# Weight preparation moved to GpSimd, one sum moved from GpSimd to VectorE, and weight loads placed otherwise, in a three-layer attention and mixing kernel

## The chip, the cores and the metric

One core of one Trainium2 chip. The metric is the device time of one execution in microseconds (us). TensorE is PE in the profile, its weight loads PEld, VectorE DVE, ScalarE ACT, GpSimd POOL, SyncE (which issues the DMAs) SP.

## What is computed

Eight batches of 576 tokens with 512 channels go through an attention with pooled keys and values, a mixing layer, and a second mixing layer, which is where the change lies:

```python
def _moe2_ref(x, w_tok1, w_tok2, w_ch1, w_ch2):     # x: 8 x 576 x 512
    xt = x.transpose(0, 2, 1)
    h = np.maximum(xt @ w_tok1, 0.0) @ w_tok2        # 576 -> 256 -> 576
    u = x + h.transpose(0, 2, 1)
    h2 = np.maximum(u @ w_ch1, 0.0) @ w_ch2          # 512 -> 1536 -> 512
    return u + h2
```

The first mixing layer ends with `u + np.maximum(u @ w_ch, 0.0)`. All weights arrive as 64-bit floats, two 32-bit words each, and are converted to fp32 by the kernel.

## The kernel before

A Tile program: instructions are written in source order, with priorities, and a scheduler places them on each engine as their inputs come ready, so that the order on an engine is not that of the source. All matrix products are made of a high and a low part of each operand (three products for one), and the two large products of the last layer use a Strassen-like scheme of seven block products, named A11, S2, A12, S1, S3, S4 and A22, so that sums and differences of the weight blocks have to be made first.

The stages, in us from the start of the span: attention and the first mixing up to about 547. From 547 to 777 the **token stage**: for each batch, eight (j, th) products with their evacuation into u on DVE (`emit_ch`, L878: relu of the product plus u), a copy of u's last 64 tokens (`dup_tail`, L536), transposes of u on PE (`emit_tr`, L173), their evacuation on ACT and DVE, and two token products (`emit_tok1`, `emit_tok2`, L927, with the store of the result to DRAM). From 777 to 1067 the **first channel product**: 36 iterations of `first_pair` (6 chunks of tokens by 6 blocks of channels), each of seven products of six matmuls. Product A11 is made in bank X and copied to p1 by ACT (L1252); S2 in Y, added to p1 by DVE as u2 (L1256); A12 is accumulated on X, its relu is the block g11 (ACT, L1260); S1 in W, copied to p5 by ACT (L1265); S3 in Z, added to p5 by DVE (L1268), then u2 added to p5 by POOL (L1269) and the relu taken by ACT (L1270); S4 on W gives g12 (L1274 DVE, L1275 ACT), A22 on Z gives g21 (L1279 DVE, L1281 ACT). Four blocks go to DRAM (L1246). Between the products, `pump` prepares operands of the next chunk: differences on DVE (L1118) and splits into high (ACT, L1114) and low parts (DVE, L1115). From 1067 to the end the second channel product.

The **weights** of the two channel products are prepared beside these stages, in steps taken by `wstep` (one after a piece of other work). `weight_steps(0, ...)` treats w_ch1 in 6 quads of 128x256 blocks, `weight_steps(1, ...)` w_ch2 in 12 quads of 128x128 blocks. A quad is: `load` (SP, L977, into ws), `conv` of its two halves from 64-bit words into wm (Abs on ACT L986, then DVE L987, L988, L992, L996), `sums` into wsum (two on POOL L1005, L1006, two on DVE L1007, L1008), `split` in two halves into wo (cast on ACT L1019, low part L1020 on POOL for the first half and on DVE for the second), and stores of wo to DRAM (L1021). The buffers of ws, wm, wsum and wo rotate over the tags given in the call; for w_ch2 each of them is one buffer (ws and wsum share the tag "kr"). The next quad's load comes after the split. `HOME_S` names the ten buffers that the evacuations of `first_pair` rotate over.

What orders the work besides priorities and the pools is only the data: a step of weights may be placed as early as its inputs are there.

## Time and profile before

| | us |
|---|---|
| median of 3 runs (lowest to highest) | 1337.89 (1337.18 to 1340.5) |
| the profiled execution | 1337.63 |
| its span | 1335.4 |
| mean granted clock of TensorE | 0.992 of 2.4 GHz |
| PE busy | 1278.4 (96%) |
| DVE, ACT, POOL busy | 970.2 (73%), 629.4 (47%), 357.9 (27%) |

The profile is of one execution. All positions are us after the start of its span, which is 2.2 us shorter than the execution's own time. Busy shares are means over stages with different limits, so a stage is read by itself: what PE does there, and what it waits for.

### The profile page before, as it was taken

Reading aid. Unit: us, or ns where it says so; the run is one execution under the profiler, and the core shown is the slowest. Engines: PE = TensorE matmul, PEld = TensorE weight load, DVE = VectorE, ACT = ScalarE, POOL = GpSimd, SP = SyncE. Lnnn points to the kernel's source line nnn. Section 1 sums busy time; section 2 is a strip of 40 time slices with the busy share of each in tenths; the row PEclk is TensorE's granted clock in tenths of the full one; section 3 lists DMA queues with packets and bytes.
Section 4 is the critical chain, followed back from the end, with each engine's and each line's share of the span. In section 5 each row is a group of like instructions: output and inputs, shape, how many; then the busy total and the mean of one; then the engine's idle time right before and its main releaser. Section 6 shows DMA issues by size and latency. Waiting matters only on the chain.

```text
span 1335.4 us, 22306 instructions
## 1 busy us (share of the span) xinstructions
PE 1278.4 (96%) x8214; PEld 1219.0 (91%) x8216; DVE 970.2 (73%) x1721; ACT 629.4 (47%) x1172; POOL 357.9 (27%) x376
## 2 busy tenths in 40 slices
...
GB/s 330 145 87 112 58 99 78 85 91 60 108 64 69 32 85 146 200 245 294 288 72 81 141 217 207 206 221 181 201 226 171 364 315 211 165 186 209 185 94 69
DMA packets 119613, 213.70 MB, mean 160 GB/s; under 512 B 11152, under 2 KB 65936, under 8 KB 119504
## 3 DMA queue, kind: packets, MB, share of 16 engines
...
HBM read 133.60 MB, written 78.64 MB: 159 GB/s over the span
## 4 chain that ended last, share of the span: by engine, by line
PE 60%; DVE 21%; issue 8%; DMA 5%; ACT 3%; POOL 3%; SPq 0%; DVEq 0%; POOLq 0%; ACTq 0%
PE x L159 22%; PE m L159 19%; PE t L159 16%; PE x L173 2%; DMA ws<-w_ch 2%; DVE sm L564 2%; DVE e L553 2%; DVE mx L552 2%; DVE tmp L736 1%; DVE sm L565 1%; POOL wo L1020 1%; DVE R L789 1%; DVE pt L605 1%; POOL wsum L1005 1%; DVE early L261 1%
## 5 line engine op out<-in xcount | busy, mean ns | idle before, releaser
L159 PE MATMUL m<-wtk,Z 128*128 128x256 f32 (+1 forms) x1536 | 247.0, 300 | 8.7 <-DVE R L789 8.3
L159 PEld LDWEIGHTS m<-wtk,Z 128*128 128x128 f32 x1536 | 217.7, 190 | 12.0 <-DVE R L789 8.7
L1269 POOL TENSOR_TENSOR p<-p,u 128x384 f32<-128x384 f32 x36 | 39.4, 1094 | 324.0 <-DVE p L1268 317.7
L751 POOL TENSOR_TENSOR Z<-tmp,Z 128x1024 fp32r<-128x1024 f32 x31 | 74.8, 2413 | 111.1 <-ACT Z L750 111.1
L159 PE MATMUL t<-wth,Xh 128*128 128x256 f32 (+1 forms) x504 | 77.1, 295 | 0.5 <-DVE Xh L536 0.2
L159 PEld LDWEIGHTS t<-wth,Xh 128*128 128x128 f32 x504 | 67.8, 190 | 4.5 <-DVE Xh L536 1.8
L718 DVE SCALAR_TENSOR_TENSOR tmp<-tmp,t 128x512 f32<-128x512 f32 x40 | 27.3, 683 | 55.3 <-ACT tmp L705 55.3
L159 PE MATMUL x<-ope_Xl,wa 128*128 128x384 f32 x336 | 65.4, 336 | 0.2 <-DVE ope_Xl L1115 0.2
L159 PE MATMUL m<-ope_Z,wa 128*128 128x384 f32 x300 | 63.7, 337 | 0.8 <-ACT ope_Z L1114 0.6
L159 PE MATMUL x<-ope_R,wa 128*128 128x384 f32 x312 | 61.8, 338 | 0.5 <-DVE p L1268 0.4
L736 DVE TENSOR_TENSOR tmp<-x,tmp 128x1024 f32<-128x1024 f32 x32 | 39.0, 1219 | 31.1 <-ACT tmp L712 16.0
L159 PE MATMUL x<-bdk,q 128*128 128x144 f32 x320 | 49.2, 309 | 11.1 <-DVE bdk L1410 6.6
L159 PEld LDWEIGHTS x<-ope_Xl,wa 128*128 128x128 f32 x336 | 58.9, 188 | 0.5 <-DVE ope_Xl L1115 0.5
L159 PEld LDWEIGHTS x<-bdk,q 128*128 128x128 f32 x320 | 46.0, 209 | 12.8 <-issue 10.8
L159 PE MATMUL m<-wtk,zt 128*128 128x256 f32 (+1 forms) x192 | 56.8, 296 | 0.0
L159 PE MATMUL x<-ope_Z,wa 128*128 128x384 f32 x276 | 55.6, 338 | 1.3 <-ACT p L1265 1.1
L159 PEld LDWEIGHTS x<-ope_R,wa 128*128 128x128 f32 x312 | 55.1, 188 | 1.2 <-DVE p L1268 1.2
L159 PE MATMUL x<-ope_Xh,wa 128*128 128x384 f32 x264 | 55.1, 341 | 0.3 <-DVE p L1268 0.2
L159 PEld LDWEIGHTS m<-ope_Z,wa 128*128 128x128 f32 x300 | 52.9, 188 | 1.8 <-ACT ope_Z L1114 0.9
L705 ACT ACTIVATE tmp<-t,magic 128x512 f32<-128x512 f32 x40 | 27.3, 684 | 57.0 <-PE t L159 44.3
L159 PE MATMUL t<-ope_Z,wa 128*128 128x384 f32 x252 | 53.6, 335 | 0.0
L569 POOL TENSOR_TENSOR e<-e,sm 128x720 f32<-128x720 f32 x32 | 45.1, 1409 | 31.6 <-DVE sm L568 31.1
...
## 6 DMA issues: line engine op xcount, KB each, us to landing
...
```

Source lines behind the costliest of these rows:

```text
L159: nc.tensor.matmul(out=o, lhsT=l, rhs=r, start=start, stop=stop, skip_group_check=skip)
L173: nc.tensor.transpose(o, i, ident)
L261: nc.vector.scalar_tensor_tensor(out=mu, in0=t[:, :, 1], scalar=0xC0000000, in1=mu, op0=ALU.bitwise_and, op1=ALU.bitwise_or,)
L552: nc.vector.tensor_reduce(out=mx[:, c0:c1, :], in_=v, axis=AX.X, op=ALU.max)
L553: nc.vector.tensor_tensor(out=e[:, c0:c1, 2 * p:2 * p + 2, :], in0=v, in1=mx[:, c0:c1, :].unsqueeze(3).to_broadcast([128, n, 2, 72]), op=A ...
L564: nc.vector.tensor_reduce(out=sm, in_=ep, axis=AX.X, op=ALU.add)
L569: nc.gpsimd.tensor_tensor(out=ep, in0=ep, in1=sm.unsqueeze(3).to_broadcast([128, 5, 2, 72]), op=ALU.mult)
L705: nc.scalar.activation(out=t, in_=pt, func=ACTF.Identity, bias=magic[:, 0:1])
L718: nc.vector.scalar_tensor_tensor(out=t, in0=t, scalar=MAGIC, in1=pt, op0=ALU.subtract, op1=ALU.subtract)
L736: nc.vector.tensor_tensor(out=tmp, in0=px.unsqueeze(1).to_broadcast([128, 2, 512]), in1=tmp, op=ALU.mult)
L751: later(1.0 if lo is nc.vector else 0.0, lambda: lo.tensor_sub(out=zl, in0=zv, in1=zh.bitcast(F32)), tg, zg)
L1269: nc.gpsimd.tensor_tensor(out=p5.t, in0=p5.t, in1=u2.t, op=ALU.add)
```

## The change

Weights: the two sums L1007 and L1008 go from DVE to POOL, and so does the low part of the second half; the casts of w_ch2 go from ACT to POOL, its Abs from ACT to DVE as a bitwise operation. The load of the next quad of w_ch2 is placed after `conv` instead of after `split`; wsum has a buffer of its own ("pl"), taken from `HOME_S`. For w_ch1 the load stays after the split, and gets a gate: POOL copies one element of the u just written into the ws tile, so that a load is behind that u. In `first_pair` the sum of p5 and u2 goes from POOL (after the Z add) to DVE (before the Z add). In the token stage the tail of u is copied by ACT instead of DVE.

Line numbers move: L977 becomes L983, L986 L993 (w_ch1) and L995 (w_ch2), L987, L988, L992, L996 become L998, L999, L1003, L1007, the sums L1005 to L1008 L1016 to L1019, the cast L1030, the low part L1031, p1's copy L1271, the u2 add L1275, the new sum of p5 L1285, the Z add L1288, its relu L1289, the g12 add L1293, the g21 add L1298.

```diff
--- before.py
+++ after.py
@@ -532,8 +532,8 @@
     pt_t = {}
     t1_t = {}
 
-    def dup_tail(t):
-        nc.vector.tensor_copy(out=t[:, :, T:TD], in_=t[:, :, 512:T])
+    def dup_tail(t, copy=nc.vector.tensor_copy):
+        copy(out=t[:, :, T:TD], in_=t[:, :, 512:T])
 
     def emit_sc(b, p):
         q = q_t[b, p // 2][:, p % 2, :]
@@ -876,8 +876,9 @@
                 i += 1
         u = u_t[b][:, j, ts]
         nc.vector.scalar_tensor_tensor(out=u, in0=o, scalar=0.0, in1=u, op0=ALU.max, op1=ALU.add)
+        gate[0] = u[0:1, 0:1]
         if j == 3 and th == 1:
-            dup_tail(u_t[b])
+            dup_tail(u_t[b], nc.scalar.copy)
 
     def emit_tr(b, c):
         u = u_t[b]
@@ -963,11 +964,16 @@
 
         def load(i):
             g, j, h = quads[i]
+            behind = gate[0]
             if whole:
                 t = ws_t([128, 2, 2, wd, 2], U32, f"ws{m}_{i}")
                 t = [t[:, kk] for kk in range(2)]
             else:
                 t = [ws_t([128, 2, wd, 2], U32, f"ws{m}_{i}_{kk}") for kk in range(2)]
+            if behind is not None:
+
+                for x in t:
+                    nc.gpsimd.tensor_copy(out=x[0:1, 0, 0:1, 0].bitcast(F32), in_=behind)
             for kk in range(2):
                 if m == 0:
                     src, r, c0 = w_ch1, (2 * kk + j) * 128, g * 256 + h * wd
@@ -983,7 +989,12 @@
             t = raw[i][0][kk]
             x = raw[i][1][:, kk]
             xu = x.bitcast(U32)
-            nc.scalar.activation(out=x, in_=t[:, :, :, 1].bitcast(F32), func=ACTF.Abs)
+            if m == 0:
+                nc.scalar.activation(out=x, in_=t[:, :, :, 1].bitcast(F32), func=ACTF.Abs)
+            else:
+                nc.vector.tensor_scalar(
+                    out=xu, in0=t[:, :, :, 1], scalar1=0x7FFFFFFF, scalar2=None, op0=ALU.bitwise_and
+                )
             nc.vector.tensor_scalar(out=x, in0=x, scalar1=F64_FLOOR, scalar2=None, op0=ALU.max)
             nc.vector.tensor_scalar(
                 out=xu, in0=xu, scalar1=3, scalar2=0x3FFFFFFF,
@@ -1004,20 +1015,20 @@
             a11, a21, a12, a22 = x[:, 0, 0], x[:, 0, 1], x[:, 1, 0], x[:, 1, 1]
             nc.gpsimd.tensor_tensor(out=s[:, 0], in0=a21, in1=a22, op=ALU.add)
             nc.gpsimd.tensor_tensor(out=s[:, 2], in0=a11, in1=a21, op=ALU.subtract)
-            nc.vector.tensor_sub(out=s[:, 1], in0=s[:, 0], in1=a11)
-            nc.vector.tensor_sub(out=s[:, 3], in0=a12, in1=s[:, 1])
+            nc.gpsimd.tensor_tensor(out=s[:, 1], in0=s[:, 0], in1=a11, op=ALU.subtract)
+            nc.gpsimd.tensor_tensor(out=s[:, 3], in0=a12, in1=s[:, 1], op=ALU.subtract)
 
         def split(i, half):
             x, s = raw[i][1:3]
-            parts = ((x[:, 1], 2, A12, nc.gpsimd), (x[:, 0, 0:1], 1, A11, nc.gpsimd)) if half == 0 else (
-                (s[:, 0:2], 2, S1, nc.vector), (s[:, 2:4], 2, S3, nc.vector))
+            parts = ((x[:, 1], 2, A12), (x[:, 0, 0:1], 1, A11)) if half == 0 else (
+                (s[:, 0:2], 2, S1), (s[:, 2:4], 2, S3))
             g, j, h = quads[i]
             if whole:
                 ow = wo_t([128, 2, 2, 2, wd], F32R, f"wo{m}_{i}_{half}")
-            for n, (src, k, o0, eng) in enumerate(parts):
+            for n, (src, k, o0) in enumerate(parts):
                 o = (ow[:, n] if whole else wo_t([128, 2, 2, wd], F32R, f"wo{m}_{i}_{half}{n}"))[:, 0:k]
-                nc.scalar.copy(out=o[:, :, 0], in_=src)
-                eng.tensor_sub(out=o[:, :, 1], in0=src, in1=o[:, :, 0].bitcast(F32))
+                (nc.scalar.copy if m == 0 else nc.gpsimd.tensor_copy)(out=o[:, :, 0], in_=src)
+                nc.gpsimd.tensor_sub(out=o[:, :, 1], in0=src, in1=o[:, :, 0].bitcast(F32))
                 nc.sync.dma_start(out=scr_w[m][:, g, o0:o0 + k, j, h * 2 * wd:(h + 1) * 2 * wd],
                                   in_=o.bitcast(F32).rearrange("p k a c -> p k (a c)"))
 
@@ -1026,17 +1037,24 @@
 
         steps = []
         for i in range(len(quads)):
+            ahead = []
             if i == 0:
                 steps += [lambda: load(0)] + [nothing] * gaps[0]
-            for f, n in ((lambda i=i: conv(i, 0), gaps[1]), (lambda i=i: conv(i, 1), gaps[2]),
-                         (lambda i=i: sums(i), gaps[3]), (lambda i=i: split(i, 0), gaps[4]),
+            if i + 1 < len(quads):
+                ahead = [lambda i=i: load(i + 1)] + [nothing] * gaps[0]
+            for f, n in ((lambda i=i: conv(i, 0), gaps[1]), (lambda i=i: conv(i, 1), gaps[2])):
+                steps += [f] + [nothing] * n
+            if m == 1:
+                steps += ahead
+            for f, n in ((lambda i=i: sums(i), gaps[3]), (lambda i=i: split(i, 0), gaps[4]),
                          (lambda i=i: split(i, 1), gaps[5])):
                 steps += [f] + [nothing] * n
-            if i + 1 < len(quads):
-                steps += [lambda i=i: load(i + 1)] + [nothing] * gaps[0]
+            if m == 0:
+                steps += ahead
         return steps
 
     wq = []
+    gate = [None]
 
     def wstep(n=1):
         while wq and n > 0:
@@ -1049,7 +1067,7 @@
     HOME_E = (("Z1", 5), ("Xh", 3), ("Xl", 3), ("R0", 3))
     HOME_O = (("R1", 3), ("e", 3), ("Z0", 5))
     HOME_R = (("n0", 1), ("n1", 1), ("n2", 1), ("n3", 1))
-    HOME_S = ["vbh", "vlh", "vbl", "vll", "bdk", "stg0", "stg1", "vlr", "t1", "pl"]
+    HOME_S = ["vbh", "vlh", "vbl", "vll", "bdk", "stg0", "stg1", "vlr", "t1"]
 
     def channel_mix():
         class Units:
@@ -1213,7 +1231,8 @@
                 mm(o, l, r, first and i == 0, last and i == len(seq) - 1, cont)
 
 
-        wq[:] = weight_steps(1, 128, (["kr"], ["n4"], ["kr"], ["vr"]), (2, 2, 2, 2, 3, 0))
+        gate[0] = None
+        wq[:] = weight_steps(1, 128, (["kr"], ["n4"], ["pl"], ["vr"]), (2, 2, 2, 2, 3, 0))
         pump(16)
         for g in range(3):
             for o in PO:
@@ -1263,10 +1282,10 @@
             prod(S1, W, True)
             p5 = evac("p5")
             nc.scalar.copy(out=p5.t, in_=W)
+            nc.vector.tensor_add(out=p5.t, in0=p5.t, in1=u2.t)
             Z = bank_any()[:, 0:NH]
             prod(S3, Z, True)
             nc.vector.tensor_add(out=p5.t, in0=Z, in1=p5.t)
-            nc.gpsimd.tensor_tensor(out=p5.t, in0=p5.t, in1=u2.t, op=ALU.add)
             nc.scalar.activation(out=p5.t, in_=p5.t, func=ACTF.Relu)
             put(3, p5)
             prod(S4, W, False)

```

Three places of the order on an engine. DVE in the token stage, the last products of batch 2 (u_6175 is its u; wm, ws, wsum and wo are weights, the first number behind the name is their quad; Xl belongs to the next batch). Before:

```order
L878 SCALAR_TENSOR_TENSOR u_6175<-x_6587,u_6175 128x256
L992 SCALAR_TENSOR_TENSOR wm_5_7482<-ws_5_1_7451,wm_5_7482 128x512
L996 SCALAR_TENSOR_TENSOR wm_5_7482<-ws_5_1_7451,wm_5_7482 128x512
L878 SCALAR_TENSOR_TENSOR u_6175<-x_6606,u_6175 128x320
L1007 TENSOR_TENSOR wsum_5_7549<-wsum_5_7549,wm_5_7482 128x256
L1008 TENSOR_TENSOR wsum_5_7549<-wm_5_7482,wsum_5_7549 128x256
L878 SCALAR_TENSOR_TENSOR u_6175<-m_6620,u_6175 128x256
L1020 TENSOR_TENSOR wo_5_10_7662<-wsum_5_7549,wo_5_10_7662 128x2x256
L878 SCALAR_TENSOR_TENSOR u_6175<-t_6639,u_6175 128x320
L865 TENSOR_TENSOR Xl<-u_6480,Xh 128x576
L536 COPY u_6175<-u_6175 128x4x64
```

and with the change:

```order
L878 SCALAR_TENSOR_TENSOR u_6175<-x_6591,u_6175 128x256
L1007 SCALAR_TENSOR_TENSOR wm_2_6571<-ws_2_0_6537,wm_2_6571 128x512
L998 TENSOR_SCALAR wm_2_6571<-wm_2_6571 128x512
L999 TENSOR_SCALAR wm_2_6571<-wm_2_6571 128x512
L878 SCALAR_TENSOR_TENSOR u_6175<-x_6610,u_6175 128x320
L1003 SCALAR_TENSOR_TENSOR wm_2_6571<-ws_2_1_6538,wm_2_6571 128x512
L1007 SCALAR_TENSOR_TENSOR wm_2_6571<-ws_2_1_6538,wm_2_6571 128x512
L878 SCALAR_TENSOR_TENSOR u_6175<-m_6624,u_6175 128x256
L878 SCALAR_TENSOR_TENSOR u_6175<-t_6643,u_6175 128x320
```

Quad 5 stood in this batch before, with its sums and low parts on DVE ahead of the last two u; now it is quad 2, of which only the conversion is on DVE, and all of it ahead of the last two u.

DVE in the first channel product, between quads 4 and 5 of w_ch2 (p_9135 is p5 of that iteration, u_9117 its u2). With the change:

```order
L1275 TENSOR_TENSOR u_9117<-t_9105,p_9103 128x384
L1003 SCALAR_TENSOR_TENSOR wm_4_9273<-ws_4_9145,wm_4_9273 128x256
L1007 SCALAR_TENSOR_TENSOR wm_4_9273<-ws_4_9145,wm_4_9273 128x256
L1285 TENSOR_TENSOR p_9135<-p_9135,u_9117 128x384
L1288 TENSOR_TENSOR p_9135<-x_9138,p_9135 128x384
L995 TENSOR_SCALAR wm_5_9485<-ws_5_9344 128x256
L1293 TENSOR_TENSOR g_9157<-x_9128,u_9117 128x384
L998 TENSOR_SCALAR wm_5_9485<-wm_5_9485 128x256
L999 TENSOR_SCALAR wm_5_9485<-wm_5_9485 128x256
L1298 TENSOR_TENSOR g_9167<-x_9138,u_9117 128x384
```

Before, quad 4's sums and low parts stood here, and the sum of p5 with u2 was not on DVE:

```order
L1256 TENSOR_TENSOR u_9269<-t_9256,p_9254 128x384
L1007 TENSOR_TENSOR wsum_4_9334<-wsum_4_9334,wm_4_9263 128x128
L1008 TENSOR_TENSOR wsum_4_9334<-wm_4_9263,wsum_4_9334 128x128
L1268 TENSOR_TENSOR p_9287<-x_9289,p_9287 128x384
L1020 TENSOR_TENSOR wo_4_1_9422<-wsum_4_9334,wo_4_1_9422 128x2x128
L1274 TENSOR_TENSOR g_9311<-x_9280,u_9269 128x384
L1020 TENSOR_TENSOR wo_4_1_9422<-wsum_4_9334,wo_4_1_9422 128x2x128
L1279 TENSOR_TENSOR g_9321<-x_9289,u_9269 128x384
```

The first operation of quad 5 (L995) now stands three rows behind the last conversion of quad 4 (L1007), ahead of both adds of the iteration's end.

POOL in the first channel product, quad 4. Before:

```order
L1269 TENSOR_TENSOR p_9204<-p_9204,u_9186 128x384
L1020 TENSOR_TENSOR wo_4_0_9370<-wm_4_9263,wo_4_0_9370 128x128
L1005 TENSOR_TENSOR wsum_4_9334<-wm_4_9263 128x128
L1006 TENSOR_TENSOR wsum_4_9334<-wm_4_9263 128x128
L1020 TENSOR_TENSOR wo_4_0_9370<-wm_4_9263,wo_4_0_9370 128x2x128
L1269 TENSOR_TENSOR p_9287<-p_9287,u_9269 128x384
```

and with the change:

```order
L1017 TENSOR_TENSOR wsum_4_9378<-wm_4_9273 128x128
L1016 TENSOR_TENSOR wsum_4_9378<-wm_4_9273 128x128
L1018 TENSOR_TENSOR wsum_4_9378<-wsum_4_9378,wm_4_9273 128x128
L1019 TENSOR_TENSOR wsum_4_9378<-wm_4_9273,wsum_4_9378 128x128
L1030 CAST wo_4_0_9416<-wm_4_9273 128x2x128
L1030 CAST wo_4_0_9416<-wm_4_9273 128x128
L1031 TENSOR_TENSOR wo_4_0_9416<-wm_4_9273,wo_4_0_9416 128x2x128
L1031 TENSOR_TENSOR wo_4_0_9416<-wm_4_9273,wo_4_0_9416 128x128
L1030 CAST wo_4_1_9466<-wsum_4_9378 128x2x128 x2
L1031 TENSOR_TENSOR wo_4_1_9466<-wsum_4_9378,wo_4_1_9466 128x2x128 x2
```

POOL has the whole quad after its conversion, and no sum of p5 between the quads.

## Rows read from the trace of the kernel before

**Rows 1.** Stage table: busy us (count) of PE, PE weight loads, DVE, ACT, POOL; granted clock, DMA share, GB/s.

```profile
613.00:618.00 5.00, 0.64 (x6) 0.41 (x5) 4.49 (x7) 2.48 (x5) 2.81 (x3) 1.00 0.33 122
618.00:622.00 4.00, 4.00 (x21) 4.00 (x21) 4.00 (x10) 4.00 (x8) 0.00 (x0) 0.57 1.02 372
...
777.00:1002.00 225.00, 211.35 (x1156) 200.73 (x1155) 160.36 (x302) 122.37 (x266) 57.02 (x73) 0.99 0.62 207
```

**Rows 2.** Waits, 500 to 777 us: waiter, releaser, us in total, times, longest.

```profile
PE t L173 <- DVE u L878: 5.2, 2, 4.4
```

**Rows 3.** Timeline near 617 us: start, duration, engine, line, operation, out<-in [idle before <-releaser].

```profile
615.06 2.13 POOL L1020 TENSOR_TENSOR wo<-wm,wo 128x256 fp32r<-128x256 f32 x2
...
616.10 1.37 DVE L1008 TENSOR_TENSOR wsum<-wm,wsum 128x256 f32<-128x256 f32 x1
...
617.86 0.33 PE L173 MATMUL t<-con,u 128*128 128x128 f32 x1 [4.36 <-DVE u L878]
```

**Rows 4.** Waits, 777 to 1067 us, those of PE.

```profile
PE m L159 <- ACT p L1252: 8.9, 16, 1.6
...
PE x L159 <- ACT p L1265: 4.1, 6, 1.8
```

**Rows 5.** Timeline, the relu L1260, five of its 36.

```profile
780.57 0.49 ACT L1260 ACTIVATE g<-m 128x384 f32<-128x384 f32 x1 [1.59 <-PE m L159]
...
805.01 0.47 ACT L1260 ACTIVATE g<-m 128x384 f32<-128x384 f32 x1
...
1002.07 0.49 ACT L1260 ACTIVATE g<-m 128x384 f32<-128x384 f32 x1
...
1032.50 0.49 ACT L1260 ACTIVATE g<-m 128x384 f32<-128x384 f32 x1 [1.55 <-PE m L159]
...
1061.77 0.49 ACT L1260 ACTIVATE g<-m 128x384 f32<-128x384 f32 x1 [1.55 <-PE m L159]
```

**Rows 6.** Timeline around 890 us, relu of p5 and PE.

```profile
891.39 0.53 ACT L1270 ACTIVATE p<-p 128x384 f32<-128x384 f32 x1 [2.25 <-POOL p L1269]
...
894.43 0.96 PE L159 MATMUL m<-ope_R,wa 128*128 128x384 f32 x4 [0.61 <-ACT p L1252]
```

**Rows 7.** Groups by form, 777 to 1000 us: busy us, mean ns | idle before, releasers.

```profile
L1270 ACT ACTIVATE p<-p 128x384 f32<-128x384 f32 x27 | 14.2, 525 | 33.0 <-POOL p L1269 33.0
...
L1019 ACT CAST wo<-wsum 128x256 fp32r<-128x256 f32 x22 | 8.2, 399 | 8.9 <-DMA scr_w<-wo 8.8
...
L1268 DVE TENSOR_TENSOR p<-x,p 128x384 f32<-128x384 f32 x27 | 15.0, 554 | 26.5 <-PE x L159 18.8 <-ACT p L1265 4.1 <-DMA ws<-w_ch 3.0
...
L1020 DVE TENSOR_TENSOR wo<-wsum,wo 128x256 fp32r<-128x256 f32 x22 | 9.6, 457 | 7.7 <-ACT wo L1019 7.7
...
L988 DVE TENSOR_SCALAR wm<-wm 128x256 uint32<-128x256 uint32 x23 | 7.6, 335 | 0.3
L1008 DVE TENSOR_TENSOR wsum<-wm,wsum 128x128 f32<-128x128 f32 x11 | 6.6, 600 | 0.3
...
L1020 POOL TENSOR_TENSOR wo<-wm,wo 128x256 fp32r<-128x256 f32 x11 | 9.3, 849 | 0.0
...
L1006 POOL TENSOR_TENSOR wsum<-wm 128x128 f32<-128x128 f32 x11 | 5.8, 526 | 0.0
```

**Rows 8.** Groups by form on POOL, whole span, one-input operations.

```profile
L574 POOL COPY pl<-e 128x80 f32<-128x80 f32 x64 | 15.5, 272 | 1.9
...
L225 POOL TENSOR_SCALAR early<-early 128x256 f32<-128x256 f32 x6 | 2.5, 418 | 4.0 <-ACT early L224 3.9
```

**Rows 9.** Timeline, POOL and DVE at 783 us and 871 to 875 us.

```profile
783.37 1.67 POOL L1269 TENSOR_TENSOR p<-p,u 128x384 f32<-128x384 f32 x1 [166.19 <-DVE p L1268]
...
871.12 0.95 DVE L1115 TENSOR_TENSOR opo_Z<-raw_n,opo_e 128x768 fp32r<-128x768 f32 x1
...
873.65 1.02 POOL L1269 TENSOR_TENSOR p<-p,u 128x384 f32<-128x384 f32 x1 [7.04 <-DVE p L1268]
874.31 1.17 DVE L1115 TENSOR_TENSOR opo_Z<-raw_n,opo_Z 128x768 fp32r<-128x768 f32 x1 [0.74 <-ACT opo_Z L1114]
```

## The prediction, made before the changed kernel was run

> **What bounds the kernel now.** I read the stage table first. PE carries every stage, and in two places it is not full [rows 1]. At 613 to 618 us it works 0.64 us of 5 while DVE works 4.49; in the 4 us after that the granted clock is 0.57, most of the time the lower of its two levels (1.2 GHz), so that PE's 4.00 busy us hold 0.57 × 4 = 2.3 us of work at full clock. And from 777 to 1002 us it works 211.35 us of 225. I then read what PE waits for. Up to 777 us it is the evacuation of u on DVE, 4.4 of 5.2 us in one piece [rows 2]. The timeline shows why: DVE is inside the weight sum L1008, 1.37 us long beside two low parts on POOL, and PE's next transpose needs a u that DVE has queued behind it [rows 3]. From 777 us on PE waits for two copies that ACT makes out of PSUM, p1 (L1252, 16 waits) and p5 (L1265, 6 waits) [rows 4].
>
> How much that stage loses is best read as a period, since waits for weight loads of PE and slow matmuls are in it too. L1260 runs once in each of the 36 iterations. From 1032.50 to 1061.77, when the weights are done and no operand is being split, four iterations take 29.27 us, 7.32 each. From 780.57 to 1061.77 there are 35 periods in 281.20 us, against 35 × 7.32 = 256.2: **25.0 us of excess** [rows 5]. The same rows tell what is not due to weights: 1002.07 to 1032.50 has no weight work but splits for the next chunk, 30.43 us for four periods, 1.15 over, and such a change of chunk comes five times (5.8 us); the opening, 780.57 to 805.01, is 24.44 for three periods, 2.5 over, most of it before weights. So about 17 us go with the weight work.
>
> How they go is in the chain around 890 us [rows 6]: ACT's relu of p5 has waited 2.25 us for POOL, which adds u2 to p5; behind the relu ACT still has casts of weights and the next relus, then comes the p1 copy, and PE has waited 0.61 us for it. The same wait of the relu is 33.0 us in 27 iterations, and ACT's casts also wait 8.8 for stores of weights [rows 7]. ACT is in order, so each of these delays the copies behind it.
>
> **The change, part by part.**
>
> *Token stage.* A quad's load now waits for the first u of its own batch, so six quads that stood together in 546 to 619 us go one to a batch. On DVE no sum or low part stands between the u any more, and the last u of the batch follows the one before it directly. This takes away the stall of 4.36 us [rows 3] and the low clock behind it, 4 × (1 − 0.57) = 1.7 us [rows 1]. The other wait for u, 5.2 − 4.4 = 0.8 us [rows 2], I leave. Against it: POOL now does all four sums and all four low parts, eight operations a batch at about 1.07 (L1020 has two in 2.13 [rows 3]), 8.5 us of a batch's (777 − 547) / 8 = 28.8. A u that DVE takes meanwhile may be late, as L1008 was; I charge 0.1 in each of six batches, 0.6. The tail copies move to ACT, which PE does not wait for there: nothing, or what a cast of 128x256 takes there (0.40 [rows 7]) once a batch. Gain **5.5**; between 2 (such waits reappear) and 7 (all go).
>
> *First channel product, ACT.* The relu no longer waits for POOL, since DVE adds u2 first (L1285): ACT loses 33.0 us of waiting and, per quad, two Abs and four casts of about 0.4, with the 8.8 of waiting for stores [rows 7]. PE waits for the p1 and p5 copies behind these, so this is where the 17 us can come back.
>
> *DVE.* Per quad it loses two sums of 0.60 and two low parts of 0.46, 2.1 us, and the wait of 7.7 for ACT's casts; it gains two bitwise operations of about 0.34 (as L988) and in each iteration an add of 0.55 (as L1268) [rows 7]; at 27 iterations to 11 quads that is 0.7 + 1.35 = 2.0. Even. But L1285 stands between the p5 copy and the Z add, and a product later PE wants the bank. A product is 7.32 / 7 = 1.046 us; of that some 0.25 is slack once copy and semaphores are paid.
>
> *POOL.* It loses 1.02 an iteration and gains two sums, two low parts and four casts per quad. A cast is not in the trace on POOL. Bounds: 0.27 (a copy of 128x80) and 0.85 (the two-input low part of the same 128x256); nearest is a one-input operation of 128x256 there, 0.42, which I take [rows 7, 8]. A quad is then 4 × 0.53 (sums) + 3 × 0.42 + 0.30 (casts) + 3 × 0.85 + 0.53 (low parts) = 6.8 us instead of 2.5. Twelve quads now end in 20 iterations, one in 20 × 7.32 / 12 = 12.2 us: POOL can carry it.
>
> *The new wait.* There is one buffer of converted weights. The next quad's first operation, now on DVE (L995), may not start before POOL has made four sums, two casts and two low parts from it: 2.1 + 0.7 + 1.4 = 4.2 us after the last conversion. Between quads 4 and 5 L995 follows that after an add, L1285 and L1288, about 2.75 us, so DVE holds with the g12 and g21 adds queued behind; ACT's relus wait for these, the next p1 copy for the relus. Walking the eleven boundaries so, four have L995 early enough to hold PE, by 0.3, 2.0, 1.25 and 1.45 us; at the others it stands behind the last add of an iteration. **5.0 us**, between 0 and 11 × 2.
>
> *Beside POOL.* A two-input DVE operation with both inputs in SBUF takes longer next to POOL: L1115 takes 0.95 alone and 1.17 where it began inside POOL's 1.02 [rows 9]. L1285 is such an add. 20 iterations with weights × 0.22 = **4.4 us**, from 0 (in the slack) to 12.0 (rival C).
>
> A rule of the Trainium skill (SBUF — State Buffer, "SBUF: two separate sides") speaks against this part: a GpSimd operation that reads SBUF and a DVE operation with two SBUF inputs exclude each other for the whole instruction. By it that L1115 would have ended 0.36 + 0.95 = 1.31 us after its start. The row says 1.17: the trace bears the rule out in direction, not in full.
>
> *Loads a block ahead, nine evacuation buffers for ten.* A load has a whole split to land in. Buffers come round after more than an iteration. Nothing; a load that came late would hold L995 as above.
>
> *Sum.* Of the excess 5.8 + 2.5 + 5.0 + 4.4 = 17.7 stays, a gain of 25.0 − 17.7 = 7.3. With 5.5 that is 12.8; 1337.6 (the profiled execution) − 12.8 = 1324.8, and the median is 0.3 above that execution: **1325 us**. The stages up to 547 us and from 1067 us keep their order and time.
>
> **The rivals.** *B, faster:* neither holds nor POOL's neighbourhood cost anything, because the loads and POOL run ahead of my walk. Splits and opening remain, 8.3: gain 16.7 + 5.5 = 22.2, so 1315.7. For it: weight-free iterations show that nothing else binds PE. Against it: the single buffer.
>
> *C, hardly faster:* L1285 waits for a whole low part in each of 20 iterations, 0.85 less 0.25 of slack, 12.0 in place of 4.4, and the stage keeps 25.3 of its 25.0: 1337.6 + 0.3 − 5.5 + 0.3 = 1332.7. For it: L1008 takes 0.60 on average beside POOL, longer than the low part of twice its size (0.46) [rows 7]. Against it: 1.17. The skill's rule above, taken in full, is this case.
>
> *D, slower:* it is POOL that is stretched, and the single buffer passes this on. The add on POOL took 1.67 where DVE worked beside it and 1.02 elsewhere [rows 9]. If POOL's 4.2 us become 4.2 × 1.64 = 6.9, L995 is held 2.7 longer at each of eleven boundaries, 2.45 past the slack, 27.0 in all: 1325 + 27 = 1352. The gain is gone from 12.8 / 11 = 1.2 us a boundary. Against it: after 800 us the adds on POOL are near 1.02, and at most boundaries L995 stands late.
>
> That the change does not do what it says can be left out: in the new order the quads stand one to a batch, and L1285 stands before L1288.
>
> **How the numbers follow.** Within 0.3%, 4 us, a measurement of this kernel can hardly tell a change from none. Forecast 0.54, B 0.14, C 0.20, D 0.12. The forecast's own range is 1318 to 1332 (token 2 to 7, holds 2 to 9, POOL's neighbourhood 0 to 8, not all at one end). B widens it to 1314, C to 1338 (with the token gain gone); what is left out is most of D and edges, under 2 in 10: 1314 to 1338. Faster (under 1333.9): 0.54 + 0.14 + 0.08 of C = 0.76; same 0.13; slower 0.11 of D.
>
> **What would show it.** Right: no wait of PE for L878 over 2 us and no granted clock under 0.9 near 617 us; periods of L1260 between 7.4 and 8.5 through iteration 20 and 7.3 to 7.6 after; ACT's relu of p5 (L1289) nearly without wait; L995 waiting 1 to 2 us for POOL at some four boundaries. Wrong: PE waiting for the Z add (L1288) in most iterations up to 20 (C); casts on POOL near 0.85 or POOL's sums near 0.9, and L995 waiting at all boundaries (D); PE full from 800 us (B); or waits for u that come back in every batch.

## The result, and the profile after

The changed kernel took 1353.09 us (median of 4 runs, 1346.97 to 1356.63) against 1337.98 before: a ratio of 1.0105, 95% interval 1.0073 to 1.0138. It is slower by 1%, where 1325 us were forecast and 1314 to 1338 given as the range.

The profiled execution is the fastest of the four, 1346.97 us, 9.3 over the profiled one of before. Three marks cut both spans alike: the first u of the token stage (L878), the first and the last relu of g11 (L1260, now L1279).

| stage, us | before | after |
|---|---|---|
| start to first u | 548.1 | 548.5 |
| first u to first relu of g11 (token stage) | 232.5 | 239.5 |
| first to last relu of g11 (channel product) | 281.2 | 283.3 |
| last relu to the end | 273.6 | 273.6 |

So 7 us were lost in the token stage and 2 in the channel product; the forecast had a gain of 5.5 and 7.3 there. The other three runs were 5 to 10 us longer still, at a granted clock of 0.989 and 0.990 instead of 0.992; they have no profile, and what else they lost stays open.

In the token stage PE no longer waits for u, as [rows 2] had it. The waits of PE from 548 to 783 us in the changed kernel:

```profile
PE x L159 <- DVE x L894: 3.7, 3, 1.9
...
PE t L159 <- DVE x L894: 2.0, 1, 2.0
PE m L159 <- DVE x L894: 2.0, 1, 2.0
...
PE x L173 <- ACT u L536: 1.8, 2, 1.4
```

It waits 7.7 us for the evacuation of the transposes (L894, added up over the three rows). The timeline of one of these waits, 585 to 590 us:

```profile
585.51 2.54 POOL L1031 TENSOR_TENSOR wo<-wsum,wo 128x512 fp32r<-128x512 f32 x2
...
586.81 1.85 DVE L865 TENSOR_TENSOR Xl<-u,Xh 128x576 fp32r<-128x576 f32 x1 [1.13 <-ACT Xh L864]
...
588.58 1.27 DVE L894 TENSOR_TENSOR x<-x,x 128x512 fp32r<-128x512 f32 x2
...
589.32 0.38 PE L159 MATMUL x<-wk2a,h1a 128*128 128x256 f32 x1 [1.89 <-DVE x L894]
```

POOL is in its low parts, and DVE's low part of u (L865, both inputs in SBUF) takes 1.85 us. L894 comes behind it, and PE behind that. The low clock that [rows 1] had at 618 us stands behind this wait now (busy us of PE, PE weight loads, DVE, ACT, POOL; granted clock, DMA share, GB/s):

```profile
590.00:594.00 4.00, 4.00 (x16) 3.52 (x15) 3.94 (x9) 0.00 (x0) 0.00 (x0) 0.57 0.53 198
```

So the 1.7 us that the forecast wanted back from the clock did not come back in this execution. The groups of L865 and L878, 548 to 775 us, before (L865 alone), after, and in e14 of the experiments, which has no weight work on POOL:

```profile
L865 DVE TENSOR_TENSOR Xl<-u,Xh 128x576 fp32r<-128x576 f32 x28 | 21.1, 759 | 0.0
```

```profile
L865 DVE TENSOR_TENSOR Xl<-u,Xh 128x576 fp32r<-128x576 f32 x28 | 30.2, 1089 | 9.3 <-ACT Xh L864 9.3
...
L878 DVE SCALAR_TENSOR_TENSOR u<-x,u 128x320 f32<-128x320 f32 x15 | 7.3, 484 | 6.6 <-PE x L159 6.6
```

```profile
L865 DVE TENSOR_TENSOR Xl<-u,Xh 128x576 fp32r<-128x576 f32 x28 | 20.6, 747 | 0.0
...
L878 DVE SCALAR_TENSOR_TENSOR u<-x,u 128x320 f32<-128x320 f32 x15 | 7.3, 489 | 10.8 <-PE x L159 10.6
```

The mean of L865 rises by 0.33 us in 28 operations, 9 us in all. Of these 28, 15 began inside one of POOL's operations, and all 15 were longer; 14 of the L878 began so, and none was longer. L878 has one input in PSUM.

In the channel product these waits answer to [rows 4] and [rows 7] (787 to 1075 us of the changed kernel):

```profile
POOL wo L1030 <- DMA scr_w<-wo: 52.0, 16, 6.6
ACT p L1289 <- DVE p L1288: 46.5, 32, 3.7
...
DVE wm L995 <- POOL wo L1031: 16.0, 7, 3.4
...
PE x L159 <- DVE p L1288: 11.0, 8, 3.7
...
PE m L159 <- ACT p L1271: 5.4, 5, 2.3
```

PE waits less for ACT's copies (5.4 us for p1 against 8.9 before) and now for the Z add. ACT's relu of p5 still waits 46.5 us, now for the Z add; the forecast took that wait as gone. The longest wait of PE, in the timeline from 828 to 836 us:

```profile
828.10 0.64 POOL L1030 CAST wo<-wm 128x256 fp32r<-128x256 f32 x2 [2.42 <-DMA scr_w<-wo]
828.69 1.16 POOL L1031 TENSOR_TENSOR wo<-wm,wo 128x256 fp32r<-128x256 f32 x2
...
829.88 0.29 DVE L995 TENSOR_SCALAR wm<-ws 128x256 uint32<-128x256 uint32 x1 [3.39 <-POOL wo L1031]
...
833.69 0.55 DVE L1285 TENSOR_TENSOR p<-p,u 128x384 f32<-128x384 f32 x1
...
835.23 0.55 DVE L1288 TENSOR_TENSOR p<-x,p 128x384 f32<-128x384 f32 x1
...
835.83 1.01 PE L159 MATMUL x<-ope_R,wa 128*128 128x384 f32 x2 [3.67 <-DVE p L1288]
```

POOL's cast waits for a store, its low part comes late, DVE's L995 waits 3.39 for the buffer, and the whole of DVE's order is late by it. This reads like the forecast's new wait, but not all of the 3.39 is POOL's: the quad's own load landed at 828.97, so that L995 could not have begun earlier than 0.9 us before it did. The experiments tell how much of the loss the hold is. Behind PE's wait the clock is low once more:

```profile
836.00:840.00 4.00, 4.00 (x15) 4.00 (x16) 3.04 (x6) 2.87 (x5) 3.41 (x4) 0.59 0.27 98
```

In the channel product the changed kernel has two such stretches (at 836 and 931 us), the kernel before one (at 932 us). By the forecast's own reckoning, 4 × (1 − 0.57), each is worth 1.7 us.

### The profile page after: what moved, and what is told of

It is laid out like the page before. It is cut to its first block, busy times and chain, and to the rows that moved or that the text cites. A ratio compares the mean times of both kernels' runs of the same rounds, so it can differ in the third digit from the quotient of the medians.

```text
span 1344.9 us, 22298 instructions
## 1 busy us (share of the span) xinstructions
PE 1278.9 (95%) x8214; PEld 1219.9 (91%) x8216; DVE 964.8 (72%) x1701; ACT 614.1 (46%) x1108; POOL 401.0 (30%) x470
## 5 line engine op out<-in xcount | busy, mean ns | idle before, releaser
L1370 POOL TENSOR_TENSOR o<-o,u 128x384 f32<-128x384 f32 x12 | 16.2, 1373 | 236.4 <-DVE u L1358 157.4
L1017 POOL TENSOR_TENSOR wsum<-wm 128x128 f32<-128x128 f32 (+1 forms) x18 | 10.9, 604 | 165.1 <-DVE wm L1007 164.8
```

Source lines behind the costliest of these rows:

```text
L1017: nc.gpsimd.tensor_tensor(out=s[:, 2], in0=a11, in1=a21, op=ALU.subtract)
L1370: nc.gpsimd.tensor_tensor(out=u22[d].t, in0=u22[d].t, in1=u2[d].t, op=ALU.add)
```

## The experiments

All are built from the kernel before or the changed one. The table has each one's stage lengths (from its profiled execution, by the marks above), its median and its ratio to the kernel before on the same chip with the 95% interval. Stage lengths are of one execution each, and they scatter: five kernels with the changed channel product (after, e1, e2, e5, e6) took 280.2 to 286.3 there, and eight with the changed token stage (after, e7 to e12, e16) took 239.0 to 242.6. So a difference of less than 6 us in the channel column, or less than 3.6 us in the token column, proves nothing by itself.

| kernel | token | channel | time | ratio |
|---|---|---|---|---|
| before | 232.5 | 281.2 | 1335.6 to 1338.0 | 1 |
| after | 239.5 | 283.3 | 1353.1 | 1.0105 (1.0073 to 1.0138) |
| e1 no gate | 237.2 | 286.3 | 1347.2 | 1.0066 (1.0046 to 1.0087) |
| e2 channel part alone | 233.4 | 281.1 | 1338.9 | 1.0020 (1.0004 to 1.0035) |
| e3 before, p5's sum on DVE | 233.7 | 277.7 | 1336.2 | 0.9995 (0.9978 to 1.0012) |
| e4 before, gate | 234.8 | 280.7 | 1340.3 | 1.0017 (0.9999 to 1.0034) |
| e5 tail copy on DVE | 240.4 | 280.2 | 1349.2 | 1.0085 (1.0056 to 1.0114) |
| e6 w_ch1 as before | 233.5 | 285.9 | 1341.6 | 1.0034 (1.0019 to 1.0048) |
| e7 two buffers, converted | 241.9 | 288.5 | 1353.8 | 1.0130 (1.0103 to 1.0157) |
| e8 three for split | 240.1 | 287.8 | 1349.7 | 1.0097 (1.0075 to 1.0120) |
| e9 e7, one load | 239.7 | 284.6 | 1350.0 | 1.0106 (1.0085 to 1.0128) |
| e10 e7, no POOL work | 240.0 | 270.4 | 1335.7 | 0.9991 (0.9976 to 1.0006) |
| e11 casts on ACT | 241.0 | 277.3 | 1341.6 | 1.0036 (1.0021 to 1.0050) |
| e12 p5's sum on POOL | 239.0 | 298.6 | 1361.0 | 1.0187 (1.0161 to 1.0213) |
| e13 before, three parts | 232.8 | 274.7 | 1332.9 | 0.9957 (0.9940 to 0.9974) |
| e14 weights and p5's sum on DVE | 223.3 | 268.6 | 1316.8 | 0.9850 (0.9834 to 0.9865) |
| e15 e14 and loads ahead | 223.3 | 271.9 | 1319.6 | 0.9873 (0.9857 to 0.9889) |
| e16 e10, POOL beside | 242.6 | 280.7 | 1346.2 | 1.0065 (1.0050 to 1.0079) |
| e17 changed, nothing on POOL | 225.5 | 268.2 | 1318.5 | 0.9867 (0.9853 to 0.9881) |
| e18 before, weights on DVE | 223.3 | 276.4 | 1325.0 | 0.9928 (0.9913 to 0.9944) |

### The token stage: e1, e4, e5, e6

e1, the changed kernel:

```diff
-        gate[0] = u[0:1, 0:1]
```

> The changed kernel without the gate: the six quads of w_ch1 are loaded as early as before, everything else as changed. Marks: the first relu of g11 (end of the token stage) was at 780.6 us before and 787.9 changed; first to last relu of g11 took 281.2 and 283.3. Theory A (the token stage lost its 7.4 us because the gate spreads POOL's sums and low parts over the batches, so that each boundary between batches meets them): the first relu comes back to 778 to 784, the later stage stays at 283 +- 3, in all some 5 us less than the changed kernel. Rival B (POOL's sums and low parts cost wherever they stand): 787 or later. Rival C (the tail copy on ACT, which PE waited for 0.45 and 1.36 us, is the loss): still above 785.

The first relu came at 786.2. Without the gate the stage still loses 4.7 us, so theory A, as it was put, falls. The value lies just under what B wanted and is what C asked for; e5 and e6 decide between these.

e4, the kernel before with the gate alone:

```diff
+        gate[0] = u[0:1, 0:1]
...
+                for x in t:
+                    nc.gpsimd.tensor_copy(out=x[0:1, 0, 0:1, 0].bitcast(F32), in_=behind)
...
+        gate[0] = None
```

> The kernel before with the gate alone: one quad of w_ch1 to a batch, sums and low parts split between POOL and DVE as before. Theory A (the token stage's loss needs POOL's whole share; the gate itself is good): first relu of g11 at 774 to 780 against 780.6, time 1331 to 1338. Rival B (spreading alone puts weight work at every boundary between batches, and PE waits there for the evacuations of the transposes): first relu at 783 or later, time over 1340.

First relu at 784.2, token stage 234.8: rival B's sign, at a third of the changed kernel's loss, and a time that can't be told from before (0.9999 to 1.0034). In place of the one long wait for u there are six of up to 1.8 us, 6.6 in all.

e5, the changed kernel:

```diff
-            dup_tail(u_t[b], nc.scalar.copy)
+            dup_tail(u_t[b])
```

> The changed kernel with one edit undone: the tail of u is copied by DVE again. From the first u of the token stage to the first relu of g11 it took 232.5 us before and 239.5 changed. Theory A (POOL's sums and low parts, which stand beside the low part Xl and the evacuation L894 on DVE at each boundary, make the loss): 238 to 240, only the two waits for the copy (1.8 us) may go. Rival C (the copy, behind casts on ACT, shifts all transposes): 235 or less.

240.4, within the scatter of the changed token stage: the copy is not it.

e6, the changed kernel with two sums and the second half's low parts of w_ch1 back on DVE:

```diff
+            sv = nc.vector if m == 0 else nc.gpsimd
-            nc.gpsimd.tensor_tensor(out=s[:, 1], ...
+            sv.tensor_tensor(out=s[:, 1], ...
...
-                nc.gpsimd.tensor_sub(out=o[:, :, 1], ...
+                (nc.vector if m == 0 and half == 1 else nc.gpsimd).tensor_sub(out=o[:, :, 1], ...
```

> The changed kernel with the sums L1018, L1019 and the low parts of the second half of w_ch1 back on DVE; gate, tail copy and all of w_ch2 as changed. Theory A (POOL's added work is the larger part of the token stage's loss; the gate alone gave 234.8): 234 to 236 from first u to first relu of g11. Rival B (spreading plus the tail on ACT make it): 238 or more. The channel product as changed, 281 to 286.

233.5: of the 7 us, 6 are POOL's added work. What gate and tail copy cost together, 1 us here, is within the scatter.

### The channel product: e2, e3, e7 to e12

e2, the changed kernel with e1's, e5's and e6's edits together.

> Only the channel product's part of the change: no gate, tail copy on DVE, and sums and low parts of w_ch1 on DVE and POOL as before. Theory A (the two parts are independent): token stage as before (first relu of g11 at 780.6 +- 1), the channel product as changed, 283 +- 4 from first to last relu against 281.2 before: time 1338 to 1346. Rival (what the token stage leaves behind disturbs the channel product, for example late loads or stores): 278 or less there, and a time under 1336.

As theory A says: the parts are independent, and the channel part by itself gains nothing.

e3, the kernel before:

```diff
             nc.scalar.copy(out=p5.t, in_=W)
+            nc.vector.tensor_add(out=p5.t, in0=p5.t, in1=u2.t)
...
-            nc.gpsimd.tensor_tensor(out=p5.t, in0=p5.t, in1=u2.t, op=ALU.add)
```

> The kernel before with one edit: u2 is added to p5 on DVE ahead of the Z add. Theory A (in the channel product the relu's wait for POOL was a main loss, and moving this sum is the good part of the change): the changed kernel's weight-free iterations show 43.6 and 36.9 us for six, splits included, so the excess of splits goes and part of the weight excess: first to last relu 268 to 275 us against 281.2, time 1325 to 1332. Rival B (the sum in front of the Z add on a loaded DVE delays the Z add as much as the relu's wait cost): 279 to 285, time within 4 us of before or slower.

277.7, between both, and no change in time: theory A promised too much. Alone, the move of this sum gives 3.5 us of the stage, within the scatter.

e7 and e8, the changed kernel with more buffers (the tag "t1" taken from the evacuations):

```diff
-        wq[:] = weight_steps(1, 128, (["kr"], ["n4"], ["pl"], ["vr"]), ...
+        wq[:] = weight_steps(1, 128, (["kr"], ["n4", "t1"], ["pl"], ["vr"]), ...
```

> The changed kernel with a second buffer for converted weights of w_ch2 (one evacuation buffer fewer). DVE's first operation of a quad waited 16.0 us in 7 for POOL to be done with the single buffer, and PE 11.0 us in 8 for the Z add behind it. Theory A (this hold is what eats the channel product's gain): the wait of L995 for POOL goes under 3 us, first to last relu of g11 falls from 283.3 to 270 to 276. Rival B (the holds only move: POOL, which waits 52 us for its stores, holds the next buffer instead, or the port does it): 279 or more.

```diff
-                ow = wo_t([128, 2, 2, 2, wd], F32R, f"wo{m}_{i}_{half}")
+                big = st("vr", [128, 2, 2, 2, wd], F32R, "wo_big")
+                parts3.extend([big[:, 0], big[:, 1], st("t1", [128, 2, 2, wd], F32R, "wo_small")])
...
```

> The changed kernel with three half-size buffers for the split weights of w_ch2 instead of one whole one (one evacuation buffer fewer). POOL's casts waited 52.0 us in 16 for stores out of that single buffer. Theory A (these waits make POOL late, and so DVE's hold): POOL's wait for stores falls under 25 us, L995's wait for POOL under 8, first to last relu of g11 to 272 to 279. Rival B (POOL's own busy time and the port are the hold): 281 or more with L995 waiting 12 us or more.

Theory A misses in both. In e7 L995's wait for POOL fell from 16.0 to 0.3 us, in e8 to 4.5, and POOL's for stores to 29.9; the channel product took 288.5 and 287.8. The holds are real, but taking them away gives nothing back: L995 waited 17.8 us for loads instead in e7, 12.3 in e8. (Both have eight evacuation buffers instead of nine. Their last stage was up to 1.3 us longer than before; in the channel product eight are no hindrance, as e10 shows with 270.4.)

e9 is e7 with the loads after the first left out:

```diff
+            if m == 1 and i > 0:
+                raw[i] = [raw[0][0], None, None]
+                return
```

> The kernel with two buffers for converted weights, and of the twelve loads of w_ch2 only the first is made: the other eleven are left out, and every quad converts the first one's words. There DVE's first operation of a quad waited 17.8 us in 16 for loads, and first to last relu of g11 took 288.5. Theory A (a first operation that is not ready and stands in DVE's order ahead of the path's adds is the loss, whether it waits for POOL or for a load): no wait of L995 left, 268 to 276 us. Rival B (DVE's own work beside POOL is the loss, waits or not): 281 or more.

284.6, in rival B's range, but not the clean case that was wanted: the wait for loads went to 0.6 us, and 9.2 us of waits for POOL came back. e10 is e7 with `sums` and `split` of w_ch2 replaced by stores from the converted words:

```diff
+            if m == 1:
+                for k, o0 in ((2, A12), (1, A11)) if half == 0 else ((2, S1), (2, S3)):
+                    nc.sync.dma_start(out=scr_w[m][...], in_=x[:, 0:k].rearrange("p k a c -> p k (a c)"))
+                return
```

> The kernel with two buffers for converted weights, with POOL's whole work on w_ch2 left out (sums, casts, low parts); the same stores are made, straight from the converted words. Theory B (POOL beside DVE's two-input operations is the loss): first to last relu of g11 266 to 274 from 288.5, and L1285 falls from 0.68 us to 0.55 on average. Theory A (waits of DVE's first operation for loads are the loss): 280 or more, with L995 still waiting 15 us or more for loads.

270.4: POOL's work is the loss, 18 us against e7, 13 against the changed kernel. L1285 took 0.555 on average. POOL's holds are gone here as well as its neighbourhood; e16 divides the two.

e11, the changed kernel:

```diff
-                (nc.scalar.copy if m == 0 else nc.gpsimd.tensor_copy)(out=o[:, :, 0], in_=src)
+                nc.scalar.copy(out=o[:, :, 0], in_=src)
```

> The changed kernel with the casts of w_ch2 on ACT again, everything else as changed. The changed order of the channel product took 280 to 286 us from first to last relu of g11 in five kernels. Theory (POOL's casts, which waited 52 us for stores, make POOL late): 272 to 279. Rival (on ACT the casts wait for the same stores, ahead of the copies of p1 and p5): 283 or more, with PE waiting for p1 and p5 copies over 10 us.

277.3, and the time 1341.6: less on POOL, less loss, as the theory says, even with the casts in ACT's order ahead of the copies. The stage alone would not prove it; the intervals of the times lie clear of each other.

e12, the changed kernel:

```diff
-            nc.vector.tensor_add(out=p5.t, in0=p5.t, in1=u2.t)
...
             nc.vector.tensor_add(out=p5.t, in0=Z, in1=p5.t)
+            nc.gpsimd.tensor_tensor(out=p5.t, in0=p5.t, in1=u2.t, op=ALU.add)
```

> The changed kernel with the sum of p5 and u2 on POOL again, after the Z add. Theory A (that sum's move is the good part of the change; on POOL it now stands behind weight work): 290 or more from first to last relu of g11, time 1356 or more. Rival B (in front of the Z add on DVE it hurts as much): 278 to 286, time as the changed kernel or less.

298.6, theory A: with weight work on POOL the sum of p5 must not stand there too; that part of the change was worth 15 us to it.

### Beside or late: e16, e14, e13, e15, e17, e18

e16 adds to e10 POOL's sums, casts and low parts of each quad again, on tiles of their own:

```diff
+                nc.gpsimd.tensor_copy(out=s[0:1, 0, 0:1], in_=x[0:1, 1, 1, 0:1])
+                nc.gpsimd.tensor_tensor(out=s[:, 1], in0=s[:, 0], in1=s[:, 2], op=ALU.add)
...
+                    nc.gpsimd.tensor_copy(out=o[:, :, 0], in_=s[:, 0:kk])
+                    nc.gpsimd.tensor_sub(out=o[:, :, 1], in0=s[:, 0:kk], in1=o[:, :, 0])
```

> The kernel without POOL's work on w_ch2 (270.4 from first to last relu of g11) with the same number and shapes of sums, casts and low parts put back on POOL, but on tiles of their own: nothing waits for them and they wait for no store; a one-element copy ties each set to its quad. Theory B (POOL beside DVE's two-input operations is the loss): 278 to 286. Theory A (POOL's lateness, through the buffers it holds and the stores it waits for, is the loss): 269 to 273. In between, the part of the 13 to 18 us that returns is the neighbourhood's.

280.7: 10.3 us return though nobody waits for POOL. Most of that is the neighbourhood; the waits for loads are only 3.0 us longer (the table below). Here are the groups on DVE from 787 to 920 us, e10 first and e16 second; the lines are those of three of the conversion's operations of a half (L995 and L998 with one input, L1003 with two), p5's sum and the Z add. In e16 they have the numbers L996, L999, L1004, L1310 and L1313:

```profile
L1293 DVE TENSOR_TENSOR p<-p,u 128x384 f32<-128x384 f32 x17 | 9.4, 555 | 13.5 <-ACT p L1292 13.4
L1296 DVE TENSOR_TENSOR p<-x,p 128x384 f32<-128x384 f32 x17 | 9.4, 555 | 1.5 <-DVE p L1293 0.5
...
L1003 DVE SCALAR_TENSOR_TENSOR wm<-ws,wm 128x256 uint32<-128x256 uint32 x22 | 9.3, 422 | 0.4
...
L995 DVE TENSOR_SCALAR wm<-ws 128x256 uint32<-128x256 uint32 x23 | 6.7, 291 | 8.8 <-DMA ws<-w_ch 5.1 <-DMA scr_g<-g 3.5
L998 DVE TENSOR_SCALAR wm<-wm 128x256 f32<-128x256 f32 x23 | 6.7, 290 | 0.4
```

```profile
L1004 DVE SCALAR_TENSOR_TENSOR wm<-ws,wm 128x256 uint32<-128x256 uint32 x20 | 10.0, 502 | 0.4
L1310 DVE TENSOR_TENSOR p<-p,u 128x384 f32<-128x384 f32 x16 | 9.7, 607 | 9.0 <-ACT p L1309 8.9
L996 DVE TENSOR_SCALAR wm<-ws 128x256 uint32<-128x256 uint32 x20 | 9.5, 473 | 9.1 <-POOL idle_w L1029 5.1 <-DMA ws<-w_ch 3.3 <-DMA scr_g<-g 0.7
...
L999 DVE TENSOR_SCALAR wm<-wm 128x256 f32<-128x256 f32 x20 | 8.9, 447 | 0.3
L1313 DVE TENSOR_TENSOR p<-x,p 128x384 f32<-128x384 f32 x16 | 8.9, 553 | 1.0
```

The one-input operations of the conversion are hit hardest (0.29 to 0.47 and 0.45), those with two inputs in SBUF less (0.42 to 0.50, 0.555 to 0.607), the Z add, from PSUM, not at all. The profile also names POOL's tile as what L996 waited for, 5.1 us in three waits. That name is wrong: in all three the quad's own load landed only then, at 826.65, 859.79 and 869.08, and L996 began 0.1 to 0.2 us later. These were waits for loads.

The table sets this beside the other kernels, from first to last relu of g11. The second column adds up what DVE's operations took above their medians in e10, e14 and e17, where POOL does no weight arithmetic; the third what the first operation of a quad waited, whatever the profile names.

| kernel | channel | DVE's operations longer by | first operation of a quad waited |
|---|---|---|---|
| after | 283.3 | 8.3 | 20.1 |
| e7 | 288.5 | 8.8 | 18.1 |
| e8 | 287.8 | 13.5 | 16.8 |
| e9 | 284.6 | 16.3 | 9.8 |
| e16 | 280.7 | 14.4 | 11.8 |
| e10 | 270.4 | 0.0 | 8.8 |
| e17 | 268.2 | 0.0 | 3.2 |

Where the waits shrink, the durations grow, and only the kernels without POOL's work have little of both. So what e16 shows for the neighbourhood is not the figure of the changed kernel, where it is 8.3 us on DVE and the rest is waiting. What the neighbourhood does to PE, in e16 at 810 us:

```profile
810.00 1.25 POOL L1030 TENSOR_TENSOR idle_w<-idle_s,idle_w 128x256 f32<-128x256 f32 x2
...
810.11 0.83 DVE L1000 TENSOR_SCALAR wm<-wm 128x256 uint32<-128x256 uint32 x1
...
811.66 0.54 DVE L1318 TENSOR_TENSOR g<-x,u 128x384 f32<-128x384 f32 x1
...
812.24 0.52 ACT L1319 ACTIVATE g<-g 128x384 f32<-128x384 f32 x1 [3.69 <-DVE g L1318]
...
813.18 0.62 PE L159 MATMUL m<-ope_Xh,wa 128*128 128x384 f32 x2 [1.67 <-ACT p L1296]
```

A shift of 0.28 us takes 0.83, the g12 add queued behind the conversion is late, ACT's relu waits 3.69 for it, the p1 copy comes behind the relu, and PE waits 1.67. (The conversion had also waited 1.01 us for its load.)

e14 goes the other way, from the kernel before: p5's sum as in e3, and

```diff
-            nc.gpsimd.tensor_tensor(out=s[:, 0], in0=a21, in1=a22, op=ALU.add)
-            nc.gpsimd.tensor_tensor(out=s[:, 2], in0=a11, in1=a21, op=ALU.subtract)
+            nc.vector.tensor_tensor(out=s[:, 0], in0=a21, in1=a22, op=ALU.add)
+            nc.vector.tensor_tensor(out=s[:, 2], in0=a11, in1=a21, op=ALU.subtract)
...
-            parts = ((x[:, 1], 2, A12, nc.gpsimd), (x[:, 0, 0:1], 1, A11, nc.gpsimd)) if half == 0 else (
+            parts = ((x[:, 1], 2, A12, nc.vector), (x[:, 0, 0:1], 1, A11, nc.vector)) if half == 0 else (
```

> The opposite of the change: the kernel before with the sum of p5 on DVE and all sums and low parts of both weights on DVE; casts and Abs on ACT, loads as before. DVE then has 2.5 us of POOL's work per quad of w_ch2 more, at its own durations some 1.3. Theory B (POOL beside DVE is the loss, not DVE's load): channel product 270 to 276, token stage under 232. Theory A (lateness of what the path's engines wait for; DVE's order is full): 278 to 285, token stage 233 or more.

Better than theory B's best: 223.3 and 268.6, 1316.8 us, 1.5% faster than the kernel before (0.9834 to 0.9865). PE waits 0.2 us in the token stage, and the granted clock stays full there. The sums of w_ch2 on DVE, which were 0.60 in [rows 7] (groups from 772 to 1000 us in e14):

```profile
L1007 DVE TENSOR_TENSOR wsum<-wsum,wm 128x128 f32<-128x128 f32 x12 | 3.4, 283 | 0.0
...
L1005 DVE TENSOR_TENSOR wsum<-wm 128x128 f32<-128x128 f32 x12 | 3.4, 282 | 0.0
...
L1008 DVE TENSOR_TENSOR wsum<-wm,wsum 128x128 f32<-128x128 f32 x12 | 3.4, 280 | 0.0
```

Four sums on DVE now take less than the two did beside POOL (4 × 0.28 against 2 × 0.60), so DVE got POOL's sums for nothing. The last sum of w_ch1, before and in e14 (groups from 548 to 775 us):

```profile
L1008 DVE TENSOR_TENSOR wsum<-wm,wsum 128x256 f32<-128x256 f32 x6 | 3.9, 654 | 0.0
```

```profile
L1008 DVE TENSOR_TENSOR wsum<-wm,wsum 128x256 f32<-128x256 f32 x6 | 2.5, 416 | 0.0
```

e13 is e3 with the Abs of w_ch2 on DVE and the load after the conversion; e15 is e14 with the same two; e17 is the changed kernel with `nc.vector` for POOL's sums and low parts and `nc.scalar.copy` for the casts; e18 is e14 with p5's sum left on POOL.

> The kernel before with three parts of the change only: the sum of p5 and u2 on DVE ahead of the Z add, the Abs of w_ch2 on DVE, the load of the next quad of w_ch2 after the conversion (wsum in a buffer of its own). Sums, low parts and casts stay where they were. Theory A (all of the loss is in what moved to POOL, and the rest is good): first to last relu of g11 268 to 275, from first u to first relu 231 to 234, time 1323 to 1331. Rival B (the good part is the sum of p5 alone, and first operations on DVE that wait for loads give it back): 276 to 281, time 1333 to 1339.

> As the kernel with all sums and low parts on DVE, and the Abs of w_ch2 on DVE and the next load after the conversion too: ACT has only casts of weights, POOL nothing. If POOL was the loss: 266 to 273 from first to last relu of g11, time 1322 to 1328. If DVE's load bounds: 280 or more.

> The changed kernel with everything that it gave to POOL, and what was there before, on DVE (sums, low parts) and ACT (casts): gate, tail copy on ACT, the sum of p5 and the Abs of w_ch2 on DVE, loads ahead stay. POOL does no weight arithmetic. If POOL beside DVE is the loss and the rest of the change is harmless: first u to first relu of g11 223 to 229, channel product 268 to 273, time 1314 to 1322. If gate and tail copy cost by themselves (0 to 3 us were seen): token stage 227 to 231, time 1320 to 1326.

> The kernel before with one thing changed: all sums and low parts of both weights on DVE; the sum of p5 stays on POOL after the Z add. Token stage as in the kernel with all on DVE, 222 to 225. Channel product: if the weights' operations beside DVE are the loss there too, 271 to 276 (with the sum of p5 on DVE too it was 268.6); if the sum of p5 on POOL, alone there, still delays ACT's relu and DVE as before, 277 to 281. Time 1318 to 1328.

e13: 274.7 in the channel product, theory A's edge, but 1332.9 us, where A wanted 1331 at most and B 1333 at least: neither. e15: 271.9 and 1319.6, as if POOL was the loss, the time a little under what was given for it. e17: 225.5, 268.2 and 1318.5: the change without POOL's work is as good as e14; the 2 us that gate and tail copy may cost in the token stage are too little to be sure of. e18: 223.3 and 276.4, the upper bound of its first case. The 9 us of the token stage are the weights' alone. Of the channel product's 12.6 us in e14, the weights alone give 4.8 (e18) and p5's sum alone 3.5 (e3); single executions scatter by as much, and together they give more than the sum of the two.

## Why the prediction was wrong

**The stall in the token stage: right that it goes, wrong in what made it.** PE's wait of 4.36 us for u went. But L1008 was long because POOL ran beside it: on DVE without POOL it needs 0.42, where [rows 3] have 1.37. The change took the sums away from DVE and made POOL run longer, where e14 leaves them on DVE, empties POOL, and loses the stall as well.

**"I charge 0.1 in each of six batches" is the step that failed there.** It gave 0.6 us to POOL's neighbourhood in the token stage; e17, the changed kernel with that work on DVE and ACT, takes 225.5 us, so that having it on POOL costs 14.0 of the 239.5. The forecast asked whether u would be late. L878, which makes u, reads PSUM and does not feel POOL (0.484 against 0.489). L865 does, and stands at each batch's boundary before the evacuations that PE needs. Counted as in the table above, DVE's operations were longer by 10.5 us in this stage before, mostly in sums and conversions; the change made that 13.1, of which 9.5 are L865's. The stage lost 7 us in place of a gain of 5.5, and e6 shows that 6 of these 7 are POOL's added work.

**"Beside POOL, 20 × 0.22 = 4.4" is the step that failed in the channel product, together with the 5.0 for the new wait.** The two gave 9.4 us to POOL's work; having it on POOL cost 15.1 (283.3 against 268.2 in e17; 12.9 against e10, which leaves it out). Of the stage's excess over 35 × 7.32 us, 27.1 stayed where the sum had 17.7. It lies where the weights are: 25.4 in the first 18 of the 35 periods, 1.8 in the other 17; in e17 it is 9.7 and 2.4. The 4.4 counted L1285 alone. That add was longer nine times, by 1.8 us in all, but DVE's other operations that read SBUF only were hit as well: all together they were longer by 8.3 us, 6.5 of it in the conversions and the splits. e16, where POOL runs free of stores, shows what this can do without any wait for POOL, up to 10.3 us of the stage for 14.4 us on DVE. How the 15.1 divide between neighbourhood, holds and the low clock behind PE's longer waits stays open. The kernel before had 16.3 us of longer operations on DVE in this stage, so the change halved that and put waits in its place.

**0.22 was no price.** In [rows 9] POOL's operation had just 0.36 us to go when L1115 began. Taken with the others of the traces it reads: the operation's own time, plus what POOL has left, less 0.13. That gives 0.95 + 0.36 − 0.13 = 1.18 (1.17), for L1008 in [rows 3], with POOL's two low parts ending at 617.19, 0.42 + 1.09 − 0.13 = 1.38 (1.37), and for the L865 above, with POOL until 588.05, 0.75 + 1.24 − 0.13 = 1.86 (1.85). All 15 of the longer L865 fit this to within 0.01 us. That L1285 came out at 0.2 each is chance. So the row did not speak against the rule of the Trainium skill (SBUF — State Buffer, "SBUF: two separate sides") that one waits out the other's whole instruction; it agrees but for 0.13 us. The same section of the Trainium skill names operations in a two-port mode beside those with two SBUF inputs, which the prediction left out; the rows of e16 for L995 and L998 fit that.

**The new wait was foreseen, and mis-sized.** L995 was held at seven boundaries, 16.0 us in all, longest 3.39, against four with 5.0 expected. For 7 of these 16.0 us the quad's own load had not landed either, and L995 waited 4.1 us more for loads by name: the nothing that the sum charged for loads a block ahead did not hold. POOL's casts took 0.48 and 0.55 for the 0.42 taken (groups of L1030, 787 to 1000 us):

```profile
L1030 POOL CAST wo<-wsum 128x256 fp32r<-128x256 f32 x24 | 12.6, 552 | 45.2 <-DMA scr_w<-wo 41.6 <-issue 3.6
...
L1030 POOL CAST wo<-wm 128x256 fp32r<-128x256 f32 x12 | 5.7, 477 | 10.5 <-DMA scr_w<-wo 10.5
```

What made POOL late was the single store buffer (52.0 us of its casts' waiting), which the sum did not charge. But e7 took the hold away and got nothing for it: L995 then waited as long for loads, and DVE's operations were longer by 8.8 us as against 8.3.

**ACT's wait was misread.** The 33.0 us of the p5 relu were taken as lost to POOL. With the sum on DVE the relu waits for the Z add instead, 46.5 us in 787 to 1075 us, and still 31.6 in e17, which has no weight work on POOL and is faster. So most of that wait was never lost to POOL. PE's waits for the two copies did fall, from 13.0 to 6.1 us.

**Right were** the period as a measure, the last stage (273.6 in both), the first, and that p5's sum on DVE is good, though how good depends on what POOL does besides: 15 us in e12, 8 in e18 against e14, 3.5 in e3. The 5.8 us of "splits" were not the splits' own: with p5's sum on DVE a chunk with splits and no weights takes 43.5 us for six, 7.25 an iteration. Even so, 12.0 us over 35 × 7.32 stay in e17, where the sum had 8.3 for splits and opening; what they are stays open.

**The rivals.** C had the mechanism in its right kind, at the wrong place: it had L1285 wait for a whole low part in each of 20 iterations, and it left the token stage its gain. That its 12.0 us are near e16's 10.3 is chance. D's time (1352) is near the median and is no hit: it has L995 held at all eleven boundaries, where it was held at seven, and its token stage gains.
